# Stores of results from GpSimd's queue instead of SyncE's, with another order of turns, in a fused attention and MLP kernel

## The chip, the core and the metric

The kernel runs on one core of a Trainium2 chip. A core has TensorE for matmuls (PE in the profile, its weight loads PEld), VectorE (DVE), ScalarE (ACT), GpSimd (POOL) and SyncE (SP), which here only issues DMAs. Each engine works through its own list of instructions in the order in which the program wrote them, and waits on semaphores for what other engines or DMAs produce. The metric is the time of one execution on the device in microseconds (us); for the kernel before it is the median of three runs.

## The reference, cut to what matters

A gated linear attention runs over 768 time steps for 4 batches and 8 heads of 48 columns. Its output, as rows of 384 columns, goes through a layer norm, a hidden layer of 1536 columns with a ReLU, a second layer, and is added to itself.

```python
for t in range(S):                      # B, H, S, D = 4, 8, 768, 48
    state = alpha[:, :, t, :, None] * state + np.einsum('bhd,bhe->bhde', k[:, :, t], v[:, :, t])
    y[:, :, t] = np.einsum('bhd,bhde->bhe', q[:, :, t], state)
x = y.transpose(0, 2, 1, 3).reshape(B, S, H * D)
xn = (x - mu) / np.sqrt(var + 1e-06) * g_ln
ch = np.maximum(xn @ w_ch1, 0.0) @ w_ch2   # 384 -> 1536 -> 384
return x + ch
```

The weights of both layers arrive as 64-bit floats and are rounded to 32 bits on the chip.

## The kernel before, in words

Time is cut into six chunks of 128 steps (c = 0 to 5), and each chunk has four batches (b = 0 to 3). The attention of one chunk and one batch is a Python generator (`attention`, line 276): gates and their products, transposes, scores, the update of the state, the output x, its layer norm and its transpose into xT. There are 24 of them. For chunks from 1 on, x is parked in DRAM (line 452) and comes back later as the tile ob (`outputs`, line 522).

The MLP takes a chunk's 512 rows (four batches) at a time, in groups of 128 hidden columns. `first` (line 590) multiplies xT with the first layer's weights into a PSUM bank hps; `top_of_hidden` (line 608, ACT), `low_of_hidden` (line 618, DVE) and `mixed_hidden` (line 627, DVE) take the ReLU and split it into parts; `second` (line 636) multiplies the parts with the second layer's weights into four accumulators ops, one per batch. The first ten groups of chunk 0 are plain fp32 matmuls; all the others use three passes of a reduced fp32, which need a third form of the first layer's weights, wmixed, added up on GpSimd (`mixed_first`, line 565) one group at a time. `results` (line 661) ends a chunk: DVE adds ops to ob (line 668), and a DMA stores ob to the output (line 669). Accumulators sit in the pool of eight PSUM banks, ob in a pool of two buffers (`KEPT`), wmixed in a pool of eight buffers that x, xn, la and parts share (`ROWS`).

Twelve pieces of weights, A to L (even ones of the first layer, odd ones of the second, each 768 KB), are loaded by SyncE (line 191), rounded by DVE and ACT (lines 193 to 212) and split (lines 226 to 233). Three buffers hold raw pieces (`STAGED`), so a fourth piece's load waits until an earlier piece has been rounded.

What sets the order of everything is the string `ORDER`: 1366 characters, each a turn, which runs one generator up to its next yield (lines 672 to 681). A turn writes its instructions at the ends of the engines' lists, so the string fixes each engine's own order; how the engines stand to each other in time is settled by the semaphores. The characters are: 0, 1, 2 and 3 for the loads of alpha, k, q and v; 4 and 5 for sums of gates and for scores; a to x for the 24 attentions (a to d are chunk 0); A to L for the twelve pieces of weights; M for `first`, R for `top_of_hidden`, N for `low_of_hidden`, V for `mixed_hidden`, Y for `second`, U for `mixed_first`, T for a third form of the second layer's weights, X for the split of xT, O for the return of x into ob, and Q for `results`. A name such as M5 or Q7 below is the fifth M or the seventh Q of a string; A5 is the fifth turn of piece A. There are 78 M turns, 62 U turns, 20 O turns and 24 Q turns (four for each chunk).

In `results` every store is issued from SyncE, but for the very last, which is cut in two halves for SyncE and ACT. SyncE also issues all loads, the parking of x, the gates' rows and the transposing DMAs. GpSimd's list holds the products with the gates (line 394, of the tiles mid and st), the additions into wmixed (line 569), some masks at the start, and one small DMA (line 302, g_ln).

Of the kernel before, what the change touches and what calls it, by code (L numbers as in the profile page):

```python
# [31 lines left out]
K = 4096.0  # L32

ORDER = (
    "0a02201baab12abba3ab0cbcbaba1cbdbAacbbbacAaa20acc1cddcdbba0bacbBC3ababaedadfbdAd"
    "baa4hedAdg4AdB1dcM2cCBBfReMCcfCehddfdRccdcccg2Cee1ecdffBfMcgBdYBggYe3cdhfhE5eREe"
    "ghfMeEffheAREdhCg30fMgRfh3MdDRCMXFRf5DfBffFigMDRhDeMMj3X2RFeDR1eeXe4fhiEhYGEXYMh"
    "j0GeijghXRgihikFFGG1hgGMjhYhGjeHHXYYjRIYjHYgjehYliYYIIHJggigiEHjIMigJXR4IjekJMMR"
    "lCKli32ffMKJ0RhhhKKXXe3egghLYRKKhU5fLAiUjh2YLjgjljMllkffAgglLiRg10NkkfkYjLjkLnMj"
    "GkYTVRNlmXT1YjkXXjlVDYjXXlXi4iXmiXkYmU32YQiFQnXj5illMjUUki00mmUki3QQkUlmiljkknTR"  # L40
    "mMpnlRMNNnokklkinn4mlRVOllplkinMYNjDTikU1VVIYJYJ2nInYRNmm0YHkYpFYVMlYT5RN3jmmnir"
    "H3ji0MmYp1mpmRNlUllkmVqmTjmlVYMYRN3lnYkUVo3m1YT22YnpnlUMnkoMoimmkppTRooUR1oU2Uko"
    "pNVNVYYYYXonnMnnnRNV0m34rXMqRXNqqMRVtN0YVXoYYpOXXYXnmsYqXXY5QQoUUmoUoOppoMrqrrMo"
    "RONQpopmoVoMqroRNVUorYqYYYrrqooooRNqprMQYRNVpppp0pnnnppYU45VtYYU1rtMRN11prUMso2R"
    "VNVY332Y3vYYpttUUUpqntrrqMtsRN2MVOtRYNpVoYsrYsrrrnrrMUUsRYqtNVmsYYMnq00sRNOMY1rV"
    "uRNtpqUYMXsVX2sXrXXURYNYY0VYXXXqQQqXq5qrqsO4sOuqusUtvsMtuqRv1w33tMtsQQxqtRNMrstN"
    "uRssNs4tYv23tVYUtuVOssvYtu2xvYvvYtVvYUMRN3VMRNq1YYxuVrsuvUttYtUxxwYUMMuRRNVxNYsY"
    "5rVvUUvvusYsvYwtutwuqwwvvwwOwUuMRMsNxVRNuUxxYYVtUYYqvvUUMMRrRNNMYVRvwNVYYVYxYYXX"
    "XXXXUXuXuXQvvv5wxwwwwOMRMRNxxxUwQQMNwUVRYNYwvVYxYMYVYRNOVYvUxYwwvUwuxwwMRNuMVuRY"
    "NwQxYuuVYYMUxxuuxORUUUMxxxNxRVYNVYMYYRNYVXXYXMRMRXNVYYXXNVMYRYXNXVYYXQOUUMUMURNY"  # L50
    "VYRNVQYYMRMUNYVRYNMRVYYNYVYOQUUOQMMUURNYVYRNVYYUMURUMNVYMMMRNRRVOOOORYYYNNVVNVYY"
    "YQQQYQ"
)


# [1 line left out]
def kernel(  # L57
# [13 lines left out]
    nc = tc.nc  # L71
# [5 lines left out]
    NCB = S // P  # L77
# [583 lines left out]
    def results():  # L661
        for c in range(NCB):
            for b in range(B):
                ob, ops, to = ob_of[c, b], acc_of.pop((c, b)), out[b, c * P:(c + 1) * P]
                end = (c, b) == (NCB - 1, B - 1)
                for i, queue in enumerate((nc.sync, nc.scalar) if end else (nc.sync,)):
                    cs = slice(i * DM // 2, (i + 1) * DM // 2) if end else slice(0, DM)
                    nc.vector.tensor_add(ob[:, cs], ops[:, cs], ob[:, cs])
                    queue.dma_start(to[:, cs], ob[:, cs])
                yield  # L670
# [4 lines left out]
    turns |= {chr(ord("A") + i): take_weights(i) for i in range(len(pieces))}  # L675
    turns |= {"M": first(), "R": top_of_hidden(), "N": low_of_hidden(), "V": mixed_hidden(),
              "Y": second(), "Q": results(), "U": mixed_first(), "T": mixed_second(),
              "X": (x for c in range(NCB) for x in split_x(c))}
    with tc.manual_schedule():
# [30 lines left out]
```

## Time and profile before

| | us |
|---|---|
| median of three runs | 410.84 |
| the three runs | 410.84, 412.85, 410.31 |
| the profiled execution | 409.77 |
| its span, from the first to the last instruction | 408.1 |
| VectorE busy | 262.5 |
| ScalarE busy | 220.0 |
| GpSimd busy | 109.6 |

The profiled execution is 1.07 us under the median; outside its span lie 1.67 us. An engine's busy time leaves out its waits, and DMA-issuing instructions of SP and ACT are not counted as busy. A matmul's recorded duration includes its way through the pipeline, so recorded matmuls overlap; how many microseconds a batch of them takes is read from the chain of waits, which lists consecutive stretches of work, each released by the one before it. The median times from issue to landing are 1.9 us for the stores of ob and 6.8 us for a piece of weights.

### The profile page before, as it was taken

What the parts mean: (1) busy time and instruction counts of PE and PEld (TensorE: products, weight loads), DVE (VectorE), ACT (ScalarE), POOL (GpSimd) and SP (SyncE); (2) the same over time, 40 slices, a digit from 0 to 9 for tenths busy, and PEclk for the clock granted to TensorE, in tenths of its full rate; (3) what the DMA queues carried; (4) which work ended last, traced back from release to release, by engine and by line L of the source; (5) the groups of instructions that cost most, each with busy time, mean ns of one, the idle gap of its engine ahead of it and who ended that gap; (6) DMA issues with size and microseconds to landing.
All of it is one profiled execution on the core that took longest, in us unless ns stands there. A gap on an engine that the chain in (4) does not pass through costs nothing.

```text
span 408.1 us, 10824 instructions
## 1 busy us (share of the span) xinstructions
PE 398.0 (98%) x4418; PEld 332.6 (81%) x4418; DVE 262.5 (64%) x425; ACT 220.0 (54%) x489; POOL 109.6 (27%) x122
## 2 busy tenths in 40 slices
PE   7888999999999999999999999999999999999996
PEld 5766876556778898888889888988889889989886
DVE  4599999979897766874654576465554344543452
ACT  6788677689569584646563458463343642210120
POOL 4231022302453053212423124245022174230000
PEclk9999999999999999999999999999999999999999
DMA  6877976894967889758687846668524130111302
GB/s 212 237 260 223 336 193 221 214 306 104 214 183 241 205 200 244 165 155 215 166 227 175 198 107 210 221 134 220 112 42 137 41 116 19 40 39 40 96 0 78
DMA packets 103706, 66.81 MB, mean 164 GB/s; under 512 B 70460, under 2 KB 95676, under 8 KB 103656
## 3 DMA queue, kind: packets, MB, share of 16 engines
q1 hardware_dynamic: 103480, 66.02, 59.8%
q8 instruction: 34, 0.56, 0.6%
q14 instruction: 16, 0.13, 0.1%
q10 hardware_dynamic: 144, 0.10, 0.1%
q0 software_dynamic: 32, 0.00, 0.0%
HBM read 34.29 MB, written 20.28 MB: 134 GB/s over the span
## 4 chain that ended last, share of the span: by engine, by line
PE 93%; DVE 5%; ACT 1%; issue 1%; DVEq 0%
PE hps L603 39%; PE ops L645 38%; PE yps L424 5%; PE ups L384 3%; PE aps L517 2%; PE tps L320 2%; PE lps L501 1%; PE aps L354 1%; DVE hmixed L632 1%; PE lps L242 1%; PE xps L476 1%; PE lps L290 1%; DVE ws L209 1%; DVE w L203 1%; DVE qk L304 0%
## 5 line engine op out<-in xcount | busy, mean ns | idle before, releaser
L615 ACT ACTIVATE htop<-hps 128x512 fp32r<-128x512 f32 (+2 forms) x78 | 43.9, 563 | 121.3 <-PE hps L603 110.1
L623 DVE SCALAR_TENSOR_TENSOR hlow<-hps,htop 128x512 fp32r<-128x512 f32 x62 | 42.6, 688 | 91.0 <-ACT htop L615 91.0
L569 POOL TENSOR_TENSOR wmixed<-top,low 128x384 fp32r<-128x384 f32 x62 | 67.1, 1097 | 78.8 <-PE hps L603 36.4
L645 PE MATMUL ops<-top,htop 128*128 128x384 f32 x248 | 56.1, 341 | 0.0
L645 PE MATMUL ops<-low,hmixed 128*128 128x384 f32 x248 | 55.7, 340 | 0.3 <-DVE hmixed L632 0.3
L603 PE MATMUL hps<-xtop,top 128*128 128x512 f32 x186 | 55.1, 404 | 0.3 <-DVE st L392 0.3
L645 PE MATMUL ops<-ws,hlow 128*128 128x384 f32 x240 | 53.5, 338 | 0.0
L603 PE MATMUL hps<-xmixed,low 128*128 128x512 f32 x186 | 53.4, 395 | 0.0
L603 PE MATMUL hps<-xlow,wmixed 128*128 128x512 f32 x186 | 53.3, 395 | 0.0
L632 DVE SCALAR_TENSOR_TENSOR hmixed<-hlow,htop 128x512 fp32r<-128x512 f32 x62 | 50.4, 819 | 3.1 <-PE ops L645 0.4
L645 PEld LDWEIGHTS ops<-top,htop 128*128 128x128 f32 x248 | 44.5, 188 | 4.0 <-issue 1.2
L645 PEld LDWEIGHTS ops<-low,hmixed 128*128 128x128 f32 x248 | 44.0, 188 | 1.4 <-DVE hmixed L632 0.9
L645 PEld LDWEIGHTS ops<-ws,hlow 128*128 128x128 f32 x240 | 43.0, 188 | 0.1
L603 PEld LDWEIGHTS hps<-xmixed,low 128*128 128x128 f32 x186 | 35.0, 188 | 8.4
L603 PEld LDWEIGHTS hps<-xlow,wmixed 128*128 128x128 f32 x186 | 35.0, 188 | 8.2
L603 PEld LDWEIGHTS hps<-xtop,top 128*128 128x128 f32 x186 | 33.2, 188 | 7.4 <-DVE st L392 1.1
L394 POOL TENSOR_TENSOR st<-st,gate 112x192 f32<-112x192 f32 x16 | 19.0, 1185 | 72.1 <-DVE st L392 72.1
L335 ACT COPY planes<-qk 128x1024 uint16<-128x1024 uint16 x32 | 33.1, 1037 | 7.0 <-DVE qk L304 7.0
L394 POOL TENSOR_TENSOR mid<-mid,gate 112x192 f32<-112x192 f32 x20 | 11.6, 584 | 86.0 <-DVE mid L392 38.4
L603 PE MATMUL hps<-xT,w 128*128 128x256 f32 (+1 forms) x96 | 28.0, 439 | 0.0
L645 PE MATMUL ops<-w,htop 128*128 128x384 f32 x80 | 27.4, 490 | 0.0
L603 PEld LDWEIGHTS hps<-xT,w 128*128 128x128 f32 x96 | 17.6, 190 | 8.1 <-issue 4.8
(121 smaller groups left out, 658.8 us busy)
## 6 DMA issues: line engine op xcount, KB each, us to landing
ws<-in_moe_w_ch_dram SPq DMA_DIRECT2D x12, 768.0 KB, 6.8
sent<-planes SPq DMA_DIRECT2D x32, 256.0 KB, 2.5
vn<-in_v_dram SPq DMA_DIRECT2D x12, 384.0 KB, 4.3
kept<-x SPq DMA_DIRECT2D x20, 192.0 KB, 3.5
rq<-in_q_dram SPq DMA_DIRECT2D x16, 192.0 KB
rk<-in_k_dram SPq DMA_DIRECT2D x16, 192.0 KB, 3.2
ob<-kept SPq DMA_DIRECT2D x16, 192.0 KB, 3.4
sentx<-parts SPq DMA_DIRECT2D x16, 192.0 KB, 1.9
```

The source lines that it names most:

```text
L320: nc.tensor.transpose(tps[:, p], qk_of(c, b)[i][:, p].rearrange("p a b -> p (a b)")[:, :R], ident)
L335: part(c)(out=planes, in_=natural.rearrange("t (d w) -> t w d", w=2))
L384: nc.tensor.matmul(up[h, p], qk_of(c, b)[1][ts, p, i, :h.stop - h.start], vn[ts, i, p], start=True, stop=True)
L394: nc.gpsimd.tensor_mul(new, new, gate[:R, s].unsqueeze(2).broadcast_to([R, NP, D]))
L424: nc.tensor.matmul(yps[r][halves[s], i, p], of, by, start=not (odd and inner), stop=bool(inner or not odd), skip_group_check=bool(odd))
L517: nc.tensor.matmul(aps[halves[i ^ n], p, s], kT[rs, p, s], qT[rs, p, s], start=True, stop=True)
L569: nc.gpsimd.tensor_add(mixed_of[g], *(first_weights(w, g[1]).bitcast(FP32) for w in (top_of, low_of)))
L603: nc.tensor.matmul(hps, ws[n][:, f], xs[f][n][:, cs], start=(n == f == 0), stop=(n == len(ws) - 1 and f == NF - 1))
L615: nc.scalar.activation(out=t, in_=hps, func=AFT.Relu, scale=1.0 if g in halved else K ** -2)
L623: nc.vector.scalar_tensor_tensor(out=t, in0=hps, scalar=0.0, in1=top.bitcast(FP32), op0=AOP.max, op1=AOP.subtract)
L632: nc.vector.scalar_tensor_tensor(out=t, in0=low.bitcast(FP32), scalar=1 - K, in1=top.bitcast(FP32), op0=AOP.mult, op1=AOP.add)
L645: nc.tensor.matmul(acc_of[c, b], hidden_of[g][n + 1][:, (b - bs[0]) * P:][:, :P], by, start=(j == n == 0), stop=last)
```

## The change

The stores of chunks 0 to 4 (Q1 to Q20) are issued from GpSimd's queue; those of chunk 5 stay with SyncE, with the halves of the last on SyncE and ACT as before. And the string `ORDER` is another one nearly from its start: it has the same characters in the same numbers, so the same work, in another sequence. Nothing is computed differently, and no buffer changes its size.

```diff
--- before.py
+++ after.py
@@ -32,24 +32,24 @@
 K = 4096.0

 ORDER = (
-    "0a02201baab12abba3ab0cbcbaba1cbdbAacbbbacAaa20acc1cddcdbba0bacbBC3ababaedadfbdAd"
-    "baa4hedAdg4AdB1dcM2cCBBfReMCcfCehddfdRccdcccg2Cee1ecdffBfMcgBdYBggYe3cdhfhE5eREe"
-    "ghfMeEffheAREdhCg30fMgRfh3MdDRCMXFRf5DfBffFigMDRhDeMMj3X2RFeDR1eeXe4fhiEhYGEXYMh"
-    "j0GeijghXRgihikFFGG1hgGMjhYhGjeHHXYYjRIYjHYgjehYliYYIIHJggigiEHjIMigJXR4IjekJMMR"
-    "lCKli32ffMKJ0RhhhKKXXe3egghLYRKKhU5fLAiUjh2YLjgjljMllkffAgglLiRg10NkkfkYjLjkLnMj"
-    "GkYTVRNlmXT1YjkXXjlVDYjXXlXi4iXmiXkYmU32YQiFQnXj5illMjUUki00mmUki3QQkUlmiljkknTR"
-    "mMpnlRMNNnokklkinn4mlRVOllplkinMYNjDTikU1VVIYJYJ2nInYRNmm0YHkYpFYVMlYT5RN3jmmnir"
-    "H3ji0MmYp1mpmRNlUllkmVqmTjmlVYMYRN3lnYkUVo3m1YT22YnpnlUMnkoMoimmkppTRooUR1oU2Uko"
-    "pNVNVYYYYXonnMnnnRNV0m34rXMqRXNqqMRVtN0YVXoYYpOXXYXnmsYqXXY5QQoUUmoUoOppoMrqrrMo"
-    "RONQpopmoVoMqroRNVUorYqYYYrrqooooRNqprMQYRNVpppp0pnnnppYU45VtYYU1rtMRN11prUMso2R"
-    "VNVY332Y3vYYpttUUUpqntrrqMtsRN2MVOtRYNpVoYsrYsrrrnrrMUUsRYqtNVmsYYMnq00sRNOMY1rV"
-    "uRNtpqUYMXsVX2sXrXXURYNYY0VYXXXqQQqXq5qrqsO4sOuqusUtvsMtuqRv1w33tMtsQQxqtRNMrstN"
-    "uRssNs4tYv23tVYUtuVOssvYtu2xvYvvYtVvYUMRN3VMRNq1YYxuVrsuvUttYtUxxwYUMMuRRNVxNYsY"
-    "5rVvUUvvusYsvYwtutwuqwwvvwwOwUuMRMsNxVRNuUxxYYVtUYYqvvUUMMRrRNNMYVRvwNVYYVYxYYXX"
-    "XXXXUXuXuXQvvv5wxwwwwOMRMRNxxxUwQQMNwUVRYNYwvVYxYMYVYRNOVYvUxYwwvUwuxwwMRNuMVuRY"
-    "NwQxYuuVYYMUxxuuxORUUUMxxxNxRVYNVYMYYRNYVXXYXMRMRXNVYYXXNVMYRYXNXVYYXQOUUMUMURNY"
-    "VYRNVQYYMRMUNYVRYNMRVYYNYVYOQUUOQMMUURNYVYRNVYYUMURUMNVYMMMRNRRVOOOORYYYNNVVNVYY"
-    "YQQQYQ"
+    "0aa021001baaa2bca2aCa0cdaad1bbbbbbbbd2cacefCbcc341dbacAcCeddd1bfcabbbadCa2bbaa3a"
+    "b0bddAdcafAfffccadeeaAfgAeCheecded4gcAcfccc1bhd5M2BMRRD3cc3dDhfghMgRMRhhgghf3ehB"
+    "eDggBffeB5hBfB0efgfddeCDffYYdde1gEBhefjiedYEYAEeEEh4McM3iRjFDMB2hFMEXjFFMYhFRigR"
+    "RheHRGhiiHXjjMHj1RhiGhiAeghY0eHYYYIGYMeMRYHGRiglIXkGgjgY4XIiggCKXlKflMjijRjIgMMJ"
+    "gMkKXKfRXCXXJR5KKf2gYRfJj3UhIij1ejlke0gIJUlkYlkkhUjLhgMkhRgMLNLk0ilmjfRhhY3V3UfX"
+    "LYl2XLNXjnLTYljkXYj1kjTljX0iXDX4mi2VXYj0mjYiUQQQiX5l3lmUMkikjkiEmjnilGRlMMRpknln"
+    "m2ioNnNklDlll1jkVkkknlTRFn4mM3NYR0nkYiknY3VYpIkkHTUUVYkNYVYiQYMjGRpFmmTNMRVYJNYV"
+    "UYU1lYpnJHm5ipMn0l2monk3Rl3TNlUrMVRUOkiN0ppYmYVYiYnn2onpTl1looOMRnNVYYjni1nnlmno"
+    "moUpTnUo2XUMRNVMMmXpYXYRRNVUYooYnNYnXVqY0XtXQXQmXmmm50Xnoop4rmqoMoRrnqoppprO2ooo"
+    "opMQsr4ONqp3UMm1pQVRNmp3pqvYRVmmooYNtn0pYVr1Y23qUYttqYUrMUooRNroVmporMRUNVqrYYYY"
+    "tp0pp2pttMRNMYUqsqOVYRNVYY1m5rUMMUoRNrOVYYRNUVYqYtrrUUnqptMsxrsRNrYpVYstr2suXMX3"
+    "MsrRUNVsYrrYqRNX41XXXXYVYquuqQsQXqqrsqqX5ss0vqusuOUuMMtvsRNQV1qOrtM1rrRtvvNsUUts"
+    "stMRtNvwQtqqqsVtOst4R3xussYYxUvYNuYYttVYYVsswYM2RNvVOt2vtMtYUYRNVYvYtxuusMrxrR3N"
+    "5vYxxUvuuVvUuMYwtRxMwRvqUuN3UVYYvNYswVUtrqsXUUuYwMMRNUwYVw3wYXRwMNVRNxXxVYYXYYuX"
+    "XQvQX5UuXXwwwxvxwwMuuuuxwxURNMOVvvRQYYwwwwwNUYxxxVOYMRMNYRVNvVYYYMMxxvxxxxRRNYVQ"
+    "NvvvYUwVUwuYYMMRNVYvRNUUYYVYMMUUURRNwVNYUUuxxuXUVYYYXXXMMXRXNXXRVOYNYYOXUVYQUUUM"
+    "RMQRNVNYVYMRNYYOYVYMRMURNVYUNYOOUUVYOYMQORNVMRYYNVYYMRMRNYVMMQRONMVRNVNVYYYRNVYY"
+    "YYQQQQ"
 )


@@ -663,7 +663,8 @@
             for b in range(B):
                 ob, ops, to = ob_of[c, b], acc_of.pop((c, b)), out[b, c * P:(c + 1) * P]
                 end = (c, b) == (NCB - 1, B - 1)
-                for i, queue in enumerate((nc.sync, nc.scalar) if end else (nc.sync,)):
+                queues = (nc.sync, nc.scalar) if end else (nc.gpsimd if c + 1 < NCB else nc.sync,)
+                for i, queue in enumerate(queues):
                     cs = slice(i * DM // 2, (i + 1) * DM // 2) if end else slice(0, DM)
                     nc.vector.tensor_add(ob[:, cs], ops[:, cs], ob[:, cs])
                     queue.dma_start(to[:, cs], ob[:, cs])
```

## The prediction

> **What bounds the kernel now.** I read the page first, for the engines' shares and the chain of waits.
>
> ```profile
> PE 398.0 (98%) x4418; PEld 332.6 (81%) x4418; DVE 262.5 (64%) x425; ACT 220.0 (54%) x489; POOL 109.6 (27%) x122
> PE 93%; DVE 5%; ACT 1%; issue 1%; DVEq 0%
> ```
>
> TensorE is the bound: 93% of the chain is its work, and no DMA and nothing of GpSimd stands on it. The chain in order of time shows where the other 7% lie.
>
> ```profile
> 33.15 1.96 PE tps L320 x16
> 112.07 1.02 DVE first L668 x2
> 196.20 3.29 DVE hmixed L632
> 395.58 9.16 PE ops L645 x52
> ```
>
> From 33.15 us to 404.74 us (the end of the last row) the chain is PE but for two places, 112.05 to 114.94 and 195.07 to 199.53. Whether PE stood still there, the busy times of these stretches tell.
>
> ```profile
> 33.15:404.74 371.59, 370.89 (x4076) 311.53 (x4076) 238.49 (x374) 195.05 (x432) 97.55 (x99) 1.00 0.59 157
> 112.05:114.94 2.89, 2.55 (x132) 2.17 (x131) 2.87 (x5) 2.86 (x10) 2.01 (x3) 1.00 0.74 264
> 195.07:199.53 4.46, 4.12 (x84) 3.22 (x83) 4.25 (x5) 4.23 (x13) 3.41 (x4) 1.00 0.48 147
> ```
>
> The columns are length, then busy time and count of PE, PEld, DVE, ACT and POOL, then clock, DMA share and GB/s. PE lacks 0.34 us in each of the two places, and 371.59 - 370.89 = 0.70 us in the whole stretch. It has other matmuls while the chain runs through DVE. So behind 33 us some 0.7 us can be won that the view shows (it calls a pipelined matmul busy, so somewhat more may hide in it), while a bad order can lose without limit. Only the first 33 us hold more: there PE waits for inputs, weights and DVE.
>
> **The change part by part.** First the 20 stores, off SyncE and onto GpSimd.
>
> ```profile
> SPq L669 <- DVE ob L668: 60.6, 10, 17.5
> L669 SPq DMA_DIRECT2D out_dram<-ob x16: 333/344/571, 176.9 to 378.3; - x16
> DMA to landing us min/median/max: 1.6/1.9/2.2
> ob<-kept SPq DMA_DIRECT2D x16, 192.0 KB, 3.4
> ```
>
> SyncE stands 60.6 us in front of stores, waiting for DVE's addition, and what is queued behind (loads, transposes, gates' rows) waits along; each store costs it 0.34 us to issue, 20 x 0.344 = 6.9 us in all. The change takes this away. On the path it is worth 0: no DMA is on the chain, and the two non-PE places end with DVE work.
>
> ```profile
> L302 POOL DMA_DIRECT2D small<-in_moe_g_ln_dram x1: 921/921/921, 4.1 to 4.1; - x1
> DMA to landing us min/median/max: 4.5/4.5/4.5
> L569 POOL TENSOR_TENSOR wmixed<-top,low 128x384 fp32r<-128x384 f32 x62 | 67.1, 1097 | 78.8 <-PE hps L603 36.4 <-DMA sentx<-parts 18.0 <-DVE low L232 12.1
> ```
>
> On GpSimd the trace has one DMA only, of 1.5 KB: 0.92 us of POOL and 4.5 us to landing, against 1.9 us from SyncE. The price of a 192 KB store is unknown. Its lower end is SyncE's 0.34 us of issue, its upper end as nearest row the longest POOL instruction of that kind of size, about 1.1 us; I take 0.92 us, the only DMA of this queue. 20 x 0.92 = 18.4 us bring POOL to 128 of 408 us. Queued behind each waiting store on POOL are wmixed (which PE's hps needs) and the gates' products. In the new string most U turns have room: U6 behind Q1 to Q3 serves M22, 53 turns after it; U9 behind Q4 serves M25, 14 turns after it; U45 behind Q16 has 8 turns to M61; U30 has 6 to M46, but stands 17 turns behind Q11. One is tight: Q7, U17, M33 come within ten turns ("Qsr4ONqp3UM"). M33 reads wmixed in its fourth matmul, so at worst a store of 0.92 and an addition of 1.1 us stand before it, 2.0 us less the three matmuls. That is the price if the cover goes; the cover is that Q7's sum has been complete since chunk 1's last Y, which stands before Q5, 39 turns earlier. I take 0, and 0 to 2 us for the range.
>
> The later landing matters where a buffer of ob is loaded again: the return of x (O) waits for the store. An addition, a store of 4.5 us and a load of 3.4 us make 8.5 us, against 5.9 us before. The tightest pair in the new string is Q9 to Q11, with O7 between: 30 turns with two M turns and attention's matmuls on PE. If it is late, DVE waits at Q11, and hlow and hmixed wait behind it; the cover is that DVE is busy 64% only. I take 0, up to 2.6 us.
>
> Now the string. It moves every engine's list, so I compare what stands ahead of the same point. M5 needs piece E in both. From the start to E4's last instruction the new list of DVE has one more piece of weights, two more L368, three more L392 and one more L445; ahead of M5 the new list of PE has two more Y, two more L424 batches, one more L517, one L501 and half an L384.
>
> ```profile
> L201 DVE TENSOR_SCALAR w<-ws 128x768 int32<-128x768 int32 x12 | 7.3, 609 | 3.6 <-DMA ws<-in_moe_w_ch_dram 3.6
> L203 DVE SCALAR_TENSOR_TENSOR w<-ws,w 128x768 f32<-128x768 uint32 x12 | 12.3, 1026 | 0.4
> L205 DVE TENSOR_SCALAR ws<-ws 128x768 int32<-128x768 int32 x12 | 7.3, 605 | 0.4
> L209 DVE SCALAR_TENSOR_TENSOR ws<-ws 128x768 int32<-128x768 int32 x12 | 11.9, 991 | 0.4 <-ACT ws L207 0.3
> L212 DVE TENSOR_TENSOR w<-w,ws 128x768 f32<-128x768 f32 x12 | 11.4, 950 | 0.1
> L368 DVE COPY_PREDICATED at<-consts,aps 128x512 f32<-128x512 int32 x20 | 13.8, 730 | 3.0 <-PE aps L517 3.0
> L392 DVE TENSOR_TENSOR mid<-ups,st 112x192 f32<-112x192 f32 x20 | 6.9, 348 | 5.8 <-PE ups L384 5.7
> L445 DVE SCALAR_TENSOR_TENSOR x<-yps,x 128x384 f32<-128x384 f32 x10 | 5.5, 553 | 1.1 <-ACT x L442 1.1
> ```
> ```profile
> 38.73 1.29 PE ops L645 x4
> 40.02 1.09 PE aps L517 x64
> 55.44 1.08 PE yps L424 x64
> 61.77 0.55 PE ups L384 x23
> 78.98 0.81 PE lps L501 x8
> ```
>
> DVE: 0.609 + 1.026 + 0.605 + 0.991 + 0.950 + 2 x 0.730 + 3 x 0.348 + 0.553 = 7.2 us more. PE: 2 x 1.29 + 2 x 1.08 + 1.09 + 0.81 + 0.55 = 7.2 us more. So by M5 DVE is no further behind PE than before: 0 for the lists. What remains are the waits in them. At its first piece DVE waits 3.6 us for the load (the L201 row). The first load of a piece is SyncE's 14th DMA in the old string and its 11th in the new one (0, 0, 2, 1, 0, 0, 1, a's row, 2, 2, then C1).
>
> ```profile
> 8.65 0.43 SPq L191 DMA_DIRECT2D ws<-in_moe_w_ch_dram  x1
> DMA to landing us min/median/max: 6.7/6.8/7.0
> L304 DVE TENSOR_TENSOR qk<-rk,lps 128x384 f32<-128x384 f32 x22 | 11.8, 545 | 3.2 <-ACT lps L296 2.7 <-ACT la L285 0.4
> ```
>
> At 0.43 us each it leaves 1.3 us earlier: a gain of 0 to 1.3 us. Against it stands piece B, which Y1 needs and PE's list has ahead of M5. Its load (B1, turn 130) is the fourth of three buffers, so it goes out only when C5 is done, and lands 0.4 + 6.8 = 7.2 us later. Between C5 and B2 DVE has two L398 (as long as the L392), one L479 (as L445), D's three (2.2 us), four L304 and two L368: 0.7 + 0.6 + 2.2 + 2.2 + 1.5 = 7.2 us. The cover is just as long as the landing; each microsecond of later landing is a microsecond of PE. I take a gain of 0.5 us for the start, between 1.3 and nothing, and 0 for B.
>
> Sum: 409.77 - 0.5 (start) + 0 (stores, wmixed, ob) + 0 (the two places: 0.7 us at most, and new ones are as likely) = 409.3 us for an execution like the profiled one. That one is 1.07 us under the median, so the time is 410.3 us.
>
> **One rule weighed.** A store on GpSimd is generated by its cores.
>
> ```profile
> L201 DVE TENSOR_SCALAR w<-ws x12: 546/554/982, 15.6 to 89.5; 128x768 int32<-128x768 int32 x12
> ```
>
> L201 takes 554 ns where L209 takes 991 ns for as many elements, so it runs in a doubled mode. In the old order the last one starts at 89.5 us and the first store at 112.7 us; in the new string all L201 and L205 stand ahead of Q1 too. The Trainium skill, page "SBUF — State Buffer", section "A bandwidth-pool intuition that's wrong (but worth ruling out)", says that DVE in such a mode locks GpSimd out of writing descriptors, so that a DMA of 620 ns took 3100 ns. By that rule a store beside such an instruction would cost some 2.5 us more (an estimate from that page), up to 50 us of POOL in twenty, and the sum would be higher by what PE sees of it at M33, 2.5 us. No run here shows it yet, and no such instruction is left when stores run, so it gets a part of the second rival's chance only.
>
> **The rivals.**
> - Slower, a late piece B. DVE waits at B2, and Y1 and all behind it wait, which puts the whole dense stretch later. For: the 3.6 us wait at the first piece, and the cover of 7.2 us that only equals the landing; piece D's load (A6) stands shortly before B1 in the queues. If the two share the bandwidth evenly, B takes another 6.8 us: 410.3 + 6.8 = 417.1 us. Against: the landings range from 6.7 to 7.0 us only. It decides (over 1%) from 4.1 us of delay on. Chance 0.15.
> - Slower, POOL in order. Stores that wait hold wmixed and the gates' products; M33 costs 2.0 us, Q11 2.6 us, together 414.9 us, more if the attentions' updates are held as well. For: POOL takes its list in order, and a waiting store holds all of it. Against: POOL is idle 73%. Chance 0.12.
> - Faster, the start shortens. The whole 3.6 us wait goes and the 0.7 us too: 410.8 - 4.3 = 406.5 us. Against: DVE's list up to M5 still has as much lead to make up. Chance 0.12.
> - The stores' move alone brings what SyncE lost: nothing on the path; same time as the forecast, inside it.
>
> **How the numbers follow.** The forecast has 0.61, with a range of its own from 408 to 413 us (the 1.3 us and 0.7 us below, one of M33 and Q11 above). 1% is 4.1 us, about what a measurement of this kernel tells from no change. Faster by over that: 0.12. Slower by over that: the late B and half of POOL's case, 0.15 + 0.06 = 0.21. Within: the forecast and the other half, 0.61 + 0.06 = 0.67. The range reaches from the short start, 406 us, to the late B, 416.5 us.
>
> **What would show it.** Right: PE busy without gaps from about 33 us on, POOL at about 128 us, stores of about 0.9 us on POOL, no L201 wait over 1 us behind the first. Wrong: a DVE wait for ws at the second or third piece; PE hps waiting for POOL wmixed; DVE waiting for ob<-kept; a store on POOL of 2 us and more; a dense stretch that begins 3 us earlier or later.

## The result, and the profile after

The changed kernel takes 417.23 us (median of four runs, 416.67 to 419.95) against 411.68 us for the kernel before in the same session: a ratio of 1.0147, 95% interval 1.0108 to 1.0185. The forecast was 410.3 us. The profiled execution is one of 417.2 us with a span of 415.4 us; that of the kernel before was 409.77 us, so 7.4 us have to be found. Ratios and intervals below leave out runs that were disturbed; medians are over all runs. Absolute times of the kernel before differ between sessions (410.28 to 412.53 us), so kernels are compared by ratios.

The page's engine line and the first line of its chain:

```profile
PE 400.3 (96%) x4418; PEld 334.3 (80%) x4418; DVE 270.2 (65%) x425; ACT 221.7 (53%) x489; POOL 119.7 (29%) x142
PE 89%; DVE 5%; ACT 2%; DMA 1%; issue 1%; SPq 1%; DVEq 0%; ACTq 0%
```

TensorE is still the bound, but stands a little longer. Where, the busy times by stretches tell, first of the kernel before and then of the changed one:

```profile
0.00:33.15 33.15, 27.09 (x342) 21.03 (x342) 23.38 (x50) 24.93 (x58) 12.06 (x24) 1.00 0.77 244
33.15:60.00 26.85, 26.85 (x462) 21.41 (x463) 25.36 (x45) 19.56 (x48) 3.51 (x5) 1.00 0.82 246
60.00:404.74 344.74, 344.05 (x3616) 290.12 (x3614) 213.12 (x330) 175.49 (x385) 94.04 (x94) 1.00 0.58 150
```
```profile
0.00:33.15 33.15, 26.38 (x338) 20.26 (x340) 22.71 (x49) 24.73 (x56) 12.39 (x23) 1.00 0.80 244
33.15:60.00 26.85, 25.12 (x452) 19.48 (x449) 24.05 (x41) 16.34 (x42) 4.32 (x7) 0.94 0.74 220
60.00:404.74 344.74, 341.71 (x3598) 287.75 (x3598) 221.07 (x332) 180.59 (x393) 103.02 (x114) 1.00 0.59 151
```

PE's busy time is less by 0.71, 1.73 and 2.34 us in the three stretches, together 4.8 us. And in the second the column of the granted clock says 0.94. The chain there, and the clock microsecond by microsecond:

```profile
43.15 1.00 PE aps L517 x64
44.15 0.27 PE yps L424 x15
44.41 1.73 issue
46.15 0.91 PE yps L424 x47
47.06 4.47 PE ops L645 x8
```
```profile
46.00:47.00 1.00, 0.85 (x48) 0.80 (x47) 1.00 (x3) 0.00 (x0) 0.36 (x1) 1.00 0.00 0
47.00:48.00 1.00, 1.00 (x5) 0.69 (x3) 1.00 (x3) 0.88 (x2) 0.56 (x2) 0.58 0.63 118
48.00:49.00 1.00, 1.00 (x3) 0.41 (x2) 1.00 (x3) 1.00 (x3) 0.74 (x1) 0.50 0.78 283
49.00:50.00 1.00, 1.00 (x3) 0.61 (x2) 0.96 (x2) 0.17 (x1) 0.00 (x0) 0.50 1.02 398
50.00:51.00 1.00, 1.00 (x3) 0.53 (x2) 0.97 (x2) 0.00 (x0) 0.00 (x0) 0.71 1.05 348
```

PE stops for 1.73 us in the middle of a group of 64 small matmuls, all of whose tiles it has read already. Behind the stop the clock is halved; 0.42 + 0.50 + 0.50 + 0.29 = 1.71 us of PE's work are lost to that. The stop and the half clock make 3.4 us, the other waits of the three stretches 0.71 + 2.34 us: 6.5 of the 7.4 us; the rest was not located. The list of PE's waits names the later ones, and DVE's and GpSimd's rows near 331 us show one of them:

```profile
PE ops L645 <- DVE hmixed L632: 1.9, 2, 1.5
PE yps L424 <- issue: 1.7, 1, 1.7
PE hps L603 <- DVE hlow L623: 0.5, 1, 0.5
```
```profile
331.65 3.47 DVE L632 SCALAR_TENSOR_TENSOR hmixed<-hlow,htop 128x512 fp32r<-128x512 f32 x1
```
```profile
331.01 0.58 POOL L670 DMA_DIRECT2D out_dram<-ob  x1 [16.48 <-ACT few L468]
331.61 5.34 POOL L569 TENSOR_TENSOR wmixed<-top,low 128x384 fp32r<-128x384 f32 x5
```

GpSimd stood 16.5 us before the store of Q16, then did the five wmixed additions that had gathered behind it in one go; hmixed, 0.69 us long as a rule, began 0.04 us after them and took 3.47 us, and PE waited 1.47 us for it. The wait of 0.5 us for hlow came about in the same way: a qk of 3.25 us, with two inputs in SBUF, stood ahead of it on DVE beside a run of three GpSimd instructions.

Such a hold is not new with the change. The kernel before has one too, the hmixed of 3.29 us in the chain that the prediction shows, beside three additions in a row, and no store on GpSimd:

```profile
195.98 2.95 POOL L569 TENSOR_TENSOR wmixed<-top,low 128x384 fp32r<-128x384 f32 x3
```
```profile
PE ops L645 <- DVE hmixed L632: 0.3, 1, 0.3
```

There it cost PE 0.3 us.

### The profile page after: what moved, and what is told of

It is laid out like the page before. It is cut to its first block, busy times and chain, and to the rows that moved or that the text cites. A ratio compares the mean times of both kernels' runs of the same rounds, so it can differ in the third digit from the quotient of the medians.

```text
span 415.4 us, 10839 instructions
## 1 busy us (share of the span) xinstructions
PE 400.3 (96%) x4418; PEld 334.3 (80%) x4418; DVE 270.2 (65%) x425; ACT 221.7 (53%) x489; POOL 119.7 (29%) x142
## 4 chain that ended last, share of the span: by engine, by line
PE 89%; DVE 5%; ACT 2%; DMA 1%; issue 1%; SPq 1%; DVEq 0%; ACTq 0%
PE ops L645 37%; PE hps L603 37%; PE yps L424 5%; PE ups L384 3%; PE aps L517 3%; DVE hmixed L632 1%; DMA ra<-in_alpha_dram 1%; PE lps L501 1%; DVE qk L304 1%; PE tps L320 1%; PE yps L408 1%; PE lps L242 1%; PE xps L476 1%; DVE xmixed L557 0%; ACT htop L615 0%
## 5 line engine op out<-in xcount | busy, mean ns | idle before, releaser
L569 POOL TENSOR_TENSOR wmixed<-top,low 128x384 fp32r<-128x384 f32 x62 | 68.4, 1119 | 47.4 <-PE hps L603 22.8
L670 POOL DMA_DIRECT2D out_dram<-ob x16 | 9.1, 567 | 88.0 <-DVE ob L669 71.5
L394 POOL TENSOR_TENSOR mid<-mid,gate 112x192 f32<-112x192 f32 x20 | 11.6, 582 | 65.2 <-DVE mid L392 57.1
L645 PE MATMUL ops<-w,htop 128*128 128x384 f32 x80 | 29.5, 516 | 0.0
L394 POOL TENSOR_TENSOR st<-st,gate 112x192 f32<-112x192 f32 x16 | 15.4, 963 | 47.6 <-DVE st L392 47.4
```

Source lines behind the costliest of these rows:

```text
L394: nc.gpsimd.tensor_mul(new, new, gate[:R, s].unsqueeze(2).broadcast_to([R, NP, D]))
L569: nc.gpsimd.tensor_add(mixed_of[g], *(first_weights(w, g[1]).bitcast(FP32) for w in (top_of, low_of)))
L645: nc.tensor.matmul(acc_of[c, b], hidden_of[g][n + 1][:, (b - bs[0]) * P:][:, :P], by, start=(j == n == 0), stop=last)
```

## The experiments

Two causes were suspected at first: piece B, rounded late, for the stop at 44 us; and the stores on GpSimd for the later waits. The first four kernels undo one or the other.

### The two halves of the change, each alone

The string without the queue, and the queue without the string (`nc.sync` for every store in the new string; the changed line of `results` in the old one).

> The new string as it is, with every store back on SyncE. Theory (two causes): of the 7 us that the changed kernel loses, about 4.1 us come from piece B being rounded late (PE stands 1.73 us before Y1 and then runs at a granted clock of 0.50 for some 3.4 us), and about 2 to 2.7 us from the stores on GpSimd, behind which wmixed additions gather and then hold up a DVE instruction with two SBUF inputs (hmixed of 3.47 us at 331.65, qk of 3.25 us at 248.88). So this one gives 414.5 to 415.2 us, keeps the stop and the half clock near 45 us, and loses PE's wait of 1.5 us for hmixed. Rival, the string alone costs it all: 417.2 us. Rival, the stores cost it all: 411.7 us.

> The old string, with the stores of chunks 0 to 4 on GpSimd's queue: the queue alone. Theory (two causes): no late piece B, granted clock 1.00 throughout, and only what gathers behind a waiting store; as the old string has its own places for U turns, 411.7 to 413.5 us. Rival, the stores cost it all: 417 us. Rival, the string costs it all: 411.7 us, no change.

The string alone took 426.31 us, ratio 1.040 (1.0347 to 1.0453): much worse than both together. The queue alone took 415.32 us, ratio 1.0129 (1.0087 to 1.0171). So the parts do not add: the new string needs its stores off SyncE, and the old one does not. In the string alone, PE's longest wait and the chain there:

```profile
PE aps L517 <- DMA turned<-sent: 5.4, 1, 5.4
```
```profile
249.99 0.31 SPq L669
250.30 0.06 issue
250.36 0.41 SPq L452
250.77 0.04 issue
250.81 0.03 SPq L342
250.84 0.03 issue
250.87 3.33 DMA turned<-sent
```
```profile
253.00:259.00 6.00, 4.66 (x100) 4.29 (x101) 2.51 (x5) 0.00 (x0) 0.00 (x0) 0.50 0.64 166
```

SyncE stood before the store (L669); the parking of x and the transposing DMAs were queued behind it, so that attention's scores came 5.4 us late, and PE ran at half clock afterwards. With the queue alone, the trace is one of 413.26 us, the fastest of its four runs; GpSimd stood 23 us in front of one store while PE needed what was queued behind it:

```profile
355.97 0.56 POOL L670 DMA_DIRECT2D out_dram<-ob  x1 [23.06 <-DVE ob L669]
356.55 3.90 POOL L569 TENSOR_TENSOR wmixed<-top,low 128x384 fp32r<-128x384 f32 x4
```
```profile
PE hps L603 <- POOL wmixed L569: 1.3, 1, 1.3
```

Another 0.8 us went by an hmixed of 3.45 us near 310 us.

### Piece B earlier

The turns of pieces B and D are exchanged in the first 230 turns, and B's last rounding turns stand together; once with the stores on GpSimd, once on SyncE.

```diff
-    ..."ed4gcAcfccc1bhd5M2BMRRD3cc3dDhfghMgRMRhhgghf3ehB" "eDggBffeB5hBfB0efgfddeCDff"...
+    ..."ed4gcBcfccc1bhd5M2AMRRB3cc3dBhfghMgRMRhhgghf3ehD" "eBBggDffeD5hDfB0efgfddeCff"...
```

> The changed kernel with pieces B and D exchanged in the string's first 230 turns: B's load takes the third buffer and is issued where D's was, B is rounded where D was and ends right after its fourth turn, D takes B's places. Theory: Y1 no longer waits for B, PE does not stop near 44 us by more than what the supply of its instructions takes, the granted clock stays at 1.00, and some 4.1 us come back: 413.1 us. Rival, PE's stop near 44 us has nothing to do with B (its record shows no releaser, only issue) and comes again: 415.5 to 417.2 us. Rival, D is now late instead and Y3 waits for it: 415 to 417 us.

> Both undone: pieces B and D exchanged as in the one before, and every store on SyncE. Theory: the two causes add, 417.2 - 4.1 - 2 to 2.7 = 410.4 to 411.1 us, level with the kernel before. Rival, something else of the new string costs as well: 413 us or more.

420.76 us, ratio 1.0245 (1.0188 to 1.0302), and 427.52 us, 1.0409 (1.0358 to 1.0459): B was early, and nothing was won. DVE's list is full there, so the state update of f became late instead (PE waited 0.9 us for mid), the half clock came all the same, and in the second kernel PE stopped for 2.2 us. The next try moved D's work on DVE behind as well.

```diff
-    ..."RRD3cc3dDhfghMgRMRhhgghf3ehB" "eDggBffeB5hBfB0efgfddeCDff"...
+    ..."RRB3cc3dBhfghMgRMRhhgghf3BBe" "heggffee5hDfB0fgfDddeDDCff"...
```

> The changed kernel with piece B loaded and rounded in place of D as in the earlier exchange, and D's work on DVE moved behind the state updates of the attentions e and f and the mask of h, so that DVE's list ahead of Y1 is shorter by D's 4 us. Theory (DVE's full list, not one piece alone, stops PE near 44 us): no stop of more than 1 us there, clock 1.00, 413 to 414.5 us; D, and then E, may be late for Y3 and M5 by up to 1 us each. Rival (the stop is the supply of PE's instructions): it comes again near 44 us and the time stays at 416.5 to 418 us.

420.67 us, 1.0206 (1.0155 to 1.0256), with a stop of 2.63 us in the same group of matmuls, and again with no releaser but issue. The theory of the late piece fell here.

### Stores written later into the lists

Each store is put into its queue 24 turns after its addition, or ahead of the next O, so that the queue seldom stands before it.

```diff
-                    queue.dma_start(to[:, cs], ob[:, cs])
+                    late.append((now[0] + LAG, to, ob))
...
+            while late and (turn == "O" or now[0] >= late[0][0]):
+                _, to, ob = late.pop(0)
+                nc.gpsimd.dma_start(to, ob)
```

> The changed kernel, but each store of chunks 0 to 4 is written into GpSimd's list 24 turns after its addition (or ahead of the next return of x, if that is sooner), so that GpSimd seldom stands in front of it. Theory (what a store on GpSimd costs is GpSimd's standing, behind which wmixed gathers and then holds DVE): the hmixed of 3.47 us at 331.65 and the qk of 3.25 us at 248.88 are short again, PE's waits of 1.47 and 0.52 us go, 417.2 - 2 = 415 us; the stop near 44 us and the half clock behind it stay. Rival, the issue or the descriptors cost: 417 us as before.

> The old string with stores on GpSimd, written 24 turns late in the same way. Theory (GpSimd's standing costs): PE's waits of 0.8 us near 310 us and 1.3 us near 356 us that the old string with prompt stores on GpSimd showed go, and the time is that of the kernel before, 410.3 to 411 us against 413.3 to 417.0 us with prompt stores. Rival, the issue or the descriptors on GpSimd cost: 413 to 417 us.

> The new string with all stores on SyncE, written 24 turns late. Theory (the new string with prompt stores on SyncE took 426 us because the transposes of the attention stood behind a waiting store, PE's wait of 5.4 us near 248 us and the half clock of 7 us behind it): that wait goes, and what stays is the stop near 44 us with its half clock: 414.5 to 417 us. Rival, it is SyncE's 0.33 us for each issue, or the transfer, that the new string does not bear: 424 us or more.

> The old string with its stores on SyncE, written 24 turns late. Theory (SyncE's 60.6 us in front of stores hold up nothing that PE needs in the old string): no change, 410.3 us within 1. Rival, they do hold up loads: 409 us or less.

On SyncE the new string came to 419.02 us, 1.0174 (1.0118 to 1.0230), instead of 426: the wait for the transposes is gone, as expected, but the time is above the 417 us expected. The old string on SyncE took 412.15 us, 1.0030 (1.0002 to 1.0058), so nothing was won; but in its trace SyncE still stood 49.2 us before stores instead of 60.6, so this run relieves SyncE of a small part only. On GpSimd the old string took 414.32 us, 1.0059 (1.0031 to 1.0087), about half of the queue's cost given back; PE's wait of 1.3 us for wmixed stayed, because an O turn forced that store early. The new string on GpSimd got no better, 1.0238 (1.0166 to 1.0311), from two runs of 420.05 and 423.08 us. Its one trace is of an execution of 430.88 us, so the cause is open; in that trace the later stores reached ob late, and DVE waited up to 3.4 us for `ob<-kept`, the price that the prediction had named for the reuse of ob.

### Start and rest taken apart

The first 317 turns (to just ahead of M14, the same number in both strings) of the one string, then what is left in the other's order.

> The first 317 turns of the new string (to just ahead of M14, 84 us), then the remaining turns in the old string's order; all stores on SyncE as before, none of them within those 317 turns. Theory (the start loses about 4.5 us: DVE's list is full, PE stops near 44 us and then runs at half clock): 411 + 4.5 = 415.5 us, with the stop near 44 us in its trace. Rival (the start's loss is caught up later, as PE would have waited elsewhere anyway): 411 us.

> The first 317 turns of the old string, then the remaining turns in the new string's order, with the stores of chunks 0 to 4 on GpSimd. Theory: no stop and no half clock at the start, so 417.2 - 4.5 = 412.7 us; the later 2 to 3 us of the changed kernel stay. Rival (the later part loses just as much without the late start): 415 to 417 us.

The new start alone: 416.84 us, 1.0123 (1.0076 to 1.0170). The new rest with its queue alone: 418.87 us, 1.0178 (1.0140 to 1.0217). Each loses about as much as both together, so the losses are not a sum. In the second one the wait for hmixed near 332 us is 3.35 us instead of 1.47: DVE was held through all five additions there, and the clock was 0.50 for 3.4 us behind that wait. PE came to that place 1.4 us earlier and waited longer.

### Two results turns later

Q16 is put behind V44, with U45 behind it, and Q11 behind N28.

```diff
-    ..."sRNQV1qOrtM1rrRtvvNsUUts" ... "xRRNYVQ" "NvvvYUwVUwuYY"...
+    ..."sRNV1qOrtM1rrRtvvNQsUUts" ... "xRRNYVN" "vvvYwVQUUwuYY"...
```

> The changed kernel with two results turns later: Q16 behind V44 (and U45 behind Q16), Q11 behind N28, so that GpSimd's store and the wmixed behind it start only after the DVE instruction that they held up. Theory (a DVE instruction with two SBUF inputs waits until a run of GpSimd instructions that began before it is over): the hmixed near 331 us takes 0.7 us instead of 3.47, the qk near 249 us 0.55 instead of 3.25, PE's waits there (1.47 and 0.52 us) go, 415.2 us. Rival (the long instructions have another cause): they stay long, 417 us.

426.30 us, 1.0359 (1.0296 to 1.0422). The two long instructions became short where they had been, but GpSimd now stood 18.6 us and gathered ten additions, and the next hmixed paid for them:

```profile
339.39 0.58 POOL L670 DMA_DIRECT2D out_dram<-ob  x1 [18.58 <-DVE ob L669]
339.99 9.69 POOL L569 TENSOR_TENSOR wmixed<-top,low 128x384 fp32r<-128x384 f32 x10
```
```profile
344.25 5.99 DVE L632 SCALAR_TENSOR_TENSOR hmixed<-hlow,htop 128x512 fp32r<-128x512 f32 x1
```

### What stops PE at 44 us

In eleven kernels with the new start the stop begins at the same place of PE's list, behind 1197 recorded instructions of PE and PEld, whatever DVE or SyncE do. (The last row's two kernels are described further down.) Its length differs. From the trace's records of DMA packets, its end follows a 16 KB transfer of the instruction queue:

| kernel | stop, us | from the landing of the transfer to PE's next matmul, us |
|---|---|---|
| changed kernel | 1.73 | 1.20 |
| string alone | 1.67 | 1.20 |
| B earlier, on GpSimd / on SyncE | 0.21 / 2.22 | 1.38 / 1.45 |
| D later | 2.63 | 1.41 |
| stores late, on GpSimd / on SyncE | 2.97 / 1.82 | 1.28 / 1.33 |
| new start alone | 1.93 | 1.47 |
| two results turns later | 1.82 | 1.57 |
| M between, late stores on SyncE / two stores on SyncE | 0.13 / 1.22 | 1.36 / 1.45 |

```profile
q8 instruction: 35, 0.57, 0.6%
```

The page counts 35 such transfers for the 8836 recorded instructions of PE and PEld, some 252 each. Ahead of the stop stand three groups of small matmuls in a row (ups, aps, yps: about 370 instructions in 3.1 us by the chain). The theory is that PE runs out of instructions there. Two kernels test it: one puts M3 and M4 between the groups; the other leaves the order alone and moves the border of the transfers by 124 instructions.

```diff
-    ..."3cc3dDhfghMgRMRhhgghf3ehB" "eDggBffeB5hBfB"...
+    ..."3cc3dDhfghghhgghf3ehBeDgg" "BffeMRB5MhRBfB"...
```
```diff
-    for _ in range(6):
+    for _ in range(3):
         nc.tensor.matmul(idle[:, :P], zero, zero, start=True, stop=True)
+    for _ in range(34):
+        nc.tensor.matmul(idle[:48, :48], zero[:64, :48], zero[:64, :48], start=True, stop=True)
```

> The changed kernel with M3 moved between the state products of e and f and the scores behind them, and M4 between those scores and the output of f (R3 and R4 behind them). Theory (PE runs out of instructions: three groups of small matmuls in a row use up 256 instructions faster than the next 256 are fetched, always at the same instruction of PE's list, 1197 records in): the plain matmuls between give the fetch 2.8 us more, the stop of 1.7 to 3 us near 44 us goes, and the half clock behind it: 417.2 - 1.7 - 1.7 = 413.8 us. Rival (PE waits there for data): the stop stays, 416.5 to 418 us.

> The changed kernel with its order untouched, but with the six idle matmuls at the start replaced by three of them and 34 tiny ones, which adds 124 instructions to PE's list ahead of everything else. Theory (instruction supply in blocks of 256): the border of the block moves 124 instructions ahead of where the three small groups end, its fetch is asked for earlier, and the stop goes or shrinks below 0.5 us, though every engine's work keeps its order: 413.8 us. Rival (PE waits for data, or for DVE): nothing changes, the stop begins at the same matmul, 417 us.

> The new string with stores on SyncE written 24 turns late (416.6 to 421.0 us alone), and the same 124 instructions more at the start. Theory: the stop near 44 us and its half clock go, GpSimd has no stores behind which wmixed could gather: 412 to 414 us. Rival: the shift does nothing, 416.5 to 421 us.

> The new string with stores on SyncE written 24 turns late, and M3 and M4 between the small groups. Theory: 412 to 414 us, like the shifted one; this would be the best version of the new string, and level with the kernel before at best. Rival: 416.5 to 421 us.

With M3 and M4 between, PE runs through in this trace and the clock stays at 1.00:

```profile
44.00:60.00 16.00, 16.00 (x276) 11.43 (x277) 14.89 (x26) 9.35 (x24) 3.38 (x4) 1.00 0.68 183
```

With the border moved, the stop inside the group is gone too, though no order was changed; a wait for piece B that had stood behind it shows instead, and a stop of the same kind appears at another place (aps):

```profile
PE ops L647 <- DVE w L212: 1.4, 1, 1.4
PE aps L519 <- issue: 1.3, 1, 1.3
```

That PE runs out of instructions is shown: the stop is tied to a place in the list, it ends with a transfer, and it moves when only the border moves. The new stop, 1.27 us, ends 1.37 us after such a transfer has landed. A smaller stop of the changed kernel (0.4 us at ups) is of the same kind: in the twelve kernels with the new string behind the start and an unmoved border it lies behind 4499 to 4502 recorded instructions, 13 x 254 behind the first, and ends 1.2 to 1.5 us after a landing; with the border moved it is gone.

The length goes with the transfer's start, which came 1.2 to 3.9 us after PE had begun the instruction 254 places ahead of the stop; the transfer itself took 1.1 to 1.2 us. Why it starts late was not found. Full DMA engines are not shown to be the reason: their share was 0.22 during the transfer of the changed kernel, and 0.00 during that of M between with two stores on SyncE, where the stop was 1.22 us. So M between does not cure the stop; in the trace above the instructions landed just in time, 1.4 us before PE began the one that they bring.

The time did not follow: M between gave 418.02 us, 1.0140 (1.0083 to 1.0197), no better than the changed kernel. Its waits:

```profile
PE ops L645 <- DVE hmixed L632: 3.7, 2, 3.4
PE tps L320 <- DVE qk L304: 3.6, 3, 1.7
PE ups L384 <- issue: 1.2, 1, 1.2
```

PE waits 3.4 us for hmixed instead of 1.5, and the clock is 0.50 for 3.4 us behind that; 1.2 us instead of 0.4 go at ups, and 1.3 us more for DVE near 39 us. The trace is of an execution of 422.18 us, 4.2 us over the median, in which the clock was also 0.50 from 14 to 21 us, so it shows more loss than the median has.

The shifted kernel took 424.14 us, 1.0249 (1.0188 to 1.0310); its tiny matmuls put the start back by some 4 us, so its time says little. On late SyncE stores the shifted one took 424.06 us, 1.0252 (1.0192 to 1.0312), and M between 419.21 us, 1.0122 (1.0061 to 1.0183), both above the 412 to 414 us expected.

### The hold between GpSimd and DVE, by itself, and two stores moved

Trials behind the kernel before (its own time means nothing), and M between with two of the twenty stores on SyncE.

```diff
-                queues = (nc.sync, nc.scalar) if end else (nc.gpsimd if c + 1 < NCB else nc.sync,)
+                on_sync = c + 1 == NCB or (c, b) in ((2, 2), (3, 3))
+                queues = (nc.sync, nc.scalar) if end else (nc.sync if on_sync else nc.gpsimd,)
```

> The kernel before, with trials added behind its last turn, so that its own time says nothing. In eight trials DVE first sets a tile, on which 1, 2, 4 or 8 additions of 128x384 on GpSimd wait, then copies from PSUM, then does one scalar-tensor-tensor of 128x512, with both inputs in SBUF or with one of them in PSUM. Theory (DVE's instruction with two SBUF inputs waits until GpSimd's whole run is over): with both in SBUF it ends about 0.6 us behind the run, some 1, 2, 4 and 8 us long; with one in PSUM 0.7 us whatever the run. Rival (it waits for the one GpSimd instruction in flight): at most 1.7 us for any run. In four more trials one store of 192 KB is issued on GpSimd, alone or beside six DVE instructions of the doubled kind (L201's): 0.57 us of GpSimd and some 3 us to landing alone; by the rule weighed in the prediction up to 3.1 us beside them, by the measured stores of the changed kernel no more than alone.

> The changed kernel with M3 and M4 between the small matmuls (418.0 us alone, PE's waits of 0.52 us near 253 us and 3.36 us near 335 us in its trace), and two of the twenty stores, those of Q11 and Q16, on SyncE instead of GpSimd. Theory (wmixed gathers behind a store that GpSimd stands in front of, and holds DVE's hmixed): both waits go, 418.0 - 3.9 = 414 us; what is left over the kernel before is the start. Rival (the two long DVE instructions come from wmixed alone, wherever the store is): they stay, 417 to 418 us. Rival, SyncE is held up instead, as in the new string with all stores on SyncE: PE waits for turned or ob elsewhere, 418 us or more.

```profile
L699 DVE SCALAR_TENSOR_TENSOR trialout<-trial,trial x4: 1158/1224/1247, 408.6 to 428.3; 128x512 f32<-128x512 f32 x4
L699 DVE SCALAR_TENSOR_TENSOR trialout<-trialps,trial x4: 669/674/675, 410.8 to 437.1; 128x512 f32<-128x512 f32 x4
```

With one input in PSUM the instruction takes 0.67 us beside GpSimd; with both in SBUF 1.16 to 1.25 us, behind one addition as behind eight. So the hold is real, and in the trial it needs two SBUF inputs; but there DVE came in after one addition. So the rival was right for the trial; what lets GpSimd go first three, five or six times in the kernels (3.47, 5.36 and 5.99 us) was not found. The rule in the Trainium skill, page "SBUF — State Buffer", section "Who interferes with whom", says that such a DVE instruction and a GpSimd instruction that reads SBUF exclude each other, the second blocked until the first is done; the trial agrees (1.22 against 0.67 us), the kernels' longer holds go beyond it. The four stores took 0.60 and 0.54 us of GpSimd alone and 0.76 and 0.77 us beside six DVE instructions of the doubled kind, of 0.34 us each; all landed within 2.4 us.

With the two stores on SyncE both waits went; hmixed, with no run of additions beside it, took 0.69 us:

```profile
335.19 0.69 DVE L632 SCALAR_TENSOR_TENSOR hmixed<-hlow,htop 128x512 fp32r<-128x512 f32 x1
```

The time was 414.98 us, 1.0080 (1.0048 to 1.0113): the best version of the new string, though the interval overlaps with that of M between alone. Additions still gather elsewhere (eight in a row from 337 us on). Its trace is of an execution of 418.84 us, and shows two waits in front of yps:

```profile
PE yps L424 <- POOL mid L394: 2.0, 1, 2.0
PE yps L424 <- issue: 1.2, 1, 1.2
```

The second is the stop. The first is the price of a store moved back: SyncE issued the store of Q11 at 250.74 us and the gate's columns, which GpSimd's mid needs, only behind it, at 252.14 us; in M between, with that store on GpSimd, they went out at 248.62 us. So the rival of a SyncE that is held up was right in part. No version beat the kernel before.

## Why the prediction was wrong, point by point

**The bound.** Right: TensorE, 96% busy, 89% of the chain.

**The failed step: the string.** The prediction compared the work that stands ahead of M5 on DVE and on PE, found 7.2 us more on each, and concluded "0 for the lists" and half a microsecond of gain in the waits. The chain before and after has M5's batch here:

```profile
45.41 3.92 PE hps L603 x18
```
```profile
56.98 3.22 PE hps L603 x14
```

M5 comes 11.6 us later, and 7.2 us of that are the added work, so 4.4 us are lost where 0.5 was to be won. The gain failed although its mechanism came: the first piece's load went out 1.27 us earlier (7.38 instead of 8.65 us) and DVE's wait of 3.6 us for it is gone, but PE, held by other waits, stood 0.71 us longer in the first 33 us. The larger part, 3.4 us between 44 and 51 us, is in no list of work: three groups of small matmuls side by side outran the supply of instructions, which cost a stop of 1.73 us and 1.71 us by the halved clock behind it. A count of engine time cannot show that; the number of instructions per microsecond can.

**The rival that gave 417.1 us was right by accident.** Piece B was not waited for: L201 of B began at 40.02 us without any idle time of DVE before it, and B early changed nothing. B would have cost 1.4 us, as the shifted kernel showed when the stop was gone; so DVE's full list, half of that rival's mechanism, was there behind the stop.

**Stores off SyncE, worth 0.** For the old string nothing speaks against it: its PE lacks 0.70 us in all behind 33 us, so SyncE's standing can cost little there; no run relieves SyncE alone (with late stores it still stood 49.2 us, at 1.0030). Wrong for the new one, where the same move is worth 426.31 against 417.23 us: the value of a queue's relief depends on what the string has put behind the stores, and I took it from the old string.

**wmixed behind stores, 0 with a range to 2 us.** Mis-sized, and by another way. M33, the tight place that I named, never waited. Runs of GpSimd work held DVE's hmixed, and a qk with hlow behind it, and PE's waits for hmixed and hlow came to 2.4 us in the changed kernel (1.9 and 0.5 us, against 0.3 us for hmixed before); the direct way, PE waiting for wmixed, came in the old string with 1.3 us. The hmixed of 3.29 us in the prediction's own chain was the sign that was passed over. The rival "POOL in order" gave 414.9 us and the queue alone measured 415.32 us, which is near by luck: neither M33 nor Q11, of which that sum was made, was waited for in the changed kernel.

**The price of a store.** I took 0.92 us from the only DMA of that queue; measured:

```profile
L670 POOL DMA_DIRECT2D out_dram<-ob x16: 542/572/583, 178.9 to 395.9; - x16
DMA to landing us min/median/max: 2.2/3.1/4.6
```

0.57 us and 3.1 us to landing, inside the bounds; GpSimd came to 119.7 us instead of 128. The reuse of ob cost nothing in the changed kernel, as taken; DVE waited up to 3.4 us for it in the one trace of the new string with late stores on GpSimd.

**The rule weighed** (a DVE instruction of the doubled kind locks GpSimd out of a DMA's descriptors) was not seen at its price: 0.77 us instead of 0.54 to 0.60 us in the trial, not 3.1 us. The trial does not refute it: its DVE instructions last 0.34 us each, and a lock that ends with each of them could add no more than that.

**The chances.** All causes of loss had been priced at nothing with a range, and added as if independent. The start alone costs 1.2%, the rest with its queue 1.8%, both 1.5%.

## What to carry to other kernels

Before calling a reordering free, count instructions and not only microseconds: where several groups of small matmuls become neighbours, PE can run dry of instructions, and a stop of under 2 us can be paid twice through the clock. A DMA that waits for its data should stand on a queue behind which nothing urgent is queued; on GpSimd it also bunches the work behind it, and a bunch can hold a DVE instruction with two SBUF inputs. A dense order has many such races. Where one was removed here, another wait often grew, so a fix is judged by the whole time and not by the wait that went.

## What the runs showed of the hardware

- PE's instructions arrive in transfers of 16 KB, some 252 to 254 recorded instructions each (35 transfers for 8836; two stops 13 transfers and 3302 instructions apart), and PE resumes 1.20 to 1.57 us after the one that it lacks has landed. The Trainium skill, page "Runtime: NRT & Kernel Launch", section "Instruction fetch mechanics", calls the crossing of such a border mostly hidden; here it cost 1.67 to 2.97 us in eight of the eleven kernels of the table.
- A stop of 1.73 us was followed by a granted clock of 0.50 for 3.4 us, and one of 5.4 us by 7 us of it; the kernel before, with no stop over 0.4 us behind 33 us, stayed at 1.00. Not every stop did that: after one of 1.82 us (late stores on SyncE) the clock stayed at 1.00. In the traces of twelve kernels, of either string, it was also 0.50 for 3.4 or 6.8 us somewhere between 14 and 36 us; in those of the kernel before and of the changed kernel it was not.
- A DVE instruction of 0.69 us with two SBUF inputs took up to 5.99 us beside a run of GpSimd additions; one with an input in PSUM took 0.67 us beside such a run.
